# Attention scores in quarters of the array, without padded copies of q, in a fused attention and FFN kernel

## The chip, the cores and the metric

The kernel runs on one core of a Trainium2 chip. The metric is the time of one execution on the device in microseconds, as the median of several executions. A core has five engines with a queue of instructions each: TensorE (PE: matrix products and transposes, which write to PSUM), VectorE (DVE), ScalarE (ACT), GpSimd (POOL) and SyncE (SP). GpSimd and SyncE issue the DMA transfers here; GpSimd also does a few elementwise products. Engines wait for each other by semaphores.

## The reference, cut to what matters

q, k and v are 8 batches x 8 heads x 576 positions x 64 in fp32. Attention is within chunks of 64 positions; a feed-forward network (FFN) of four weight matrices follows.

```
q_c, k_c, v_c = (t.reshape(B, H, S // 64, 64, D) for t in (q, k, v))
scores = scale * np.matmul(q_c, k_c.transpose(0, 1, 2, 4, 3))
scores = scores - np.max(scores, axis=-1, keepdims=True)
attn = np.exp(scores)
attn = attn / (np.sum(attn, axis=-1, keepdims=True) + 1e-09)
out = np.matmul(attn, v_c)
x = out.transpose(0, 2, 1, 3).reshape(4608, 512)
h = (x @ w1) * (x @ w2) @ w3          # 512 -> 1024 -> 1024
return h @ w_out                      # 4608 x 512
```

## The kernel before, in words

**Groups and tiles.** The 4608 tokens are 36 groups of 128 (two chunks of 64), and the FFN works on 9 tiles of 4 groups. Matrix operands are bf16.

**One group of attention** (`add_group`). q and k of a group are loaded side by side into a tile `raw`. They must be turned, so that the head dimension lies on partitions. `TURN_QK` says how: by a DMA transpose that SyncE issues (`qk_turn`, tile `kqT`; 25 groups), or by 16 TensorE transposes into PSUM (`t_emit`, tile `p_tr`, 64 partitions per transpose; 11 groups). On the partitions of a turned tile lie two heads, 64 rows each. To get the scores of both heads from one matmul that contracts over 128 partitions, q is copied into a padded tile `qd` (three of them, zeroed at the start): the first head's q into the upper left part, the second's into the lower right (`q_copy`, two copies per group). k is used as it was turned by DMA, or copied from `p_tr` (`k_copy`). `s_emit` then does 8 matmuls of 64 columns into one PSUM bank, `p_sc`; on its partitions are the two heads, and along the row chunk, head pair and key.

VectorE takes the maximum per row (`max_emit`). Then, for most groups, VectorE subtracts it (`sub_emit`, tile `sd`) and ScalarE takes the exponential of the whole tile; for the 13 groups in `EXP_8`, ScalarE takes it straight from PSUM in 8 instructions, one per head and chunk, with the maximum as its bias (and q was scaled when it was copied). VectorE sums and inverts, and VectorE or GpSimd normalizes into `an` (five groups on GpSimd). The probabilities are turned, by DMA for 20 groups (`at_turn`) or by 4 TensorE transposes into a bank `p_at` for 16 (`at_emit`, `TURN_A`), multiplied by v (`av_emit`, 8 matmuls into `p_av`), and copied into `xt`, the input of the FFN.

**The FFN.** w3 and w_out are multiplied first (`add_w3o`: 8 transposes of a row block of w3, then 8 matmuls, for each of 8 rows), so that the FFN has two stages: `add_tile` does 64 matmuls of 512 columns with w1 and w2, ScalarE copies one product and VectorE multiplies the two (`abT`), and then 8 matmuls per group with the product of w3 and w_out give the output.

**What sets the order.** All of these are entries of a `Plan`. It walks through time with a cost for each entry, and gives each engine the ready entry with the lowest key; `SHIFT` (four numbers per group) and `ROW_KEY` move the keys. The instruction order of every engine is fixed by that. GpSimd is the exception: it takes the loads in the order of `LOADS`, in which `("an", g)` is a normalization done by GpSimd. Until 20 us of the plan, TensorE's idle time is filled with matmuls on a zero tile (`fill`). PSUM has 8 banks: 4 for `ffn`, one each for `p_sc`, `p_at`, `p_av` and `p_tr`.

Of the kernel before, what the change touches and what calls it, by code (L numbers as in the profile page):

```python
# [21 lines left out]
LOADS = [("qk", 0), ("wo", 0, 4), ("ident",), ("qk", 1), ("w3", 7, 8), ("wo", 4, 8), ("qk", 2), ("w3", 2, 3),  # L22
# [10 lines left out]
SLACK, SLACK_FROM = 1.48611, 4  # L33

TURN_QK = [g not in (0, 1, 2, 3, 4, 5, 6, 7, 8, 9, 12,) for g in range(36)]
TURN_A = [g not in (0, 1, 2, 3, 4, 5, 6, 7, 11, 13, 14, 15, 16, 21, 25, 27,) for g in range(36)]
LATE = 5
PACKED = 0.33
SHIFT = {0: (-214, -279, -160, -174), 1: (-78, -168, -88, -40), 2: (-37, -204, -55, -133), 3: (-142, -300, -25, -102),
# [10 lines left out]
ROW_KEY = [-2.1, 1.9, -1.9, 8.1, -5.5, 1, 8.1, -2.9]  # L50
EXP_8 = (2, 4, 5, 6, 7, 9, 10, 12, 13, 14, 15, 18, 19)
# [15 lines left out]
class Plan:  # L67
# [34 lines left out]
    def run(self):  # L102
        free = {e: 0.0 for e in ("PE", "ACT", "DVE", "POOL", "SP")}
        free["POOL"] = free["SP"] = 1.2
# [60 lines left out]
def kernel(  # L165
# [19 lines left out]
    nc = tc.nc  # L185
# [17 lines left out]
    BUFS = {"raw": 6, "kqT": 4, "kT": 3, "qd": 3, "vd": 3, "sd": 2, "e": 2, "an": 4, "at": 6, "w3t": 2, "abT": 2,  # L203
            "a_sb": 3, "o_sb": 4, "ffn": 4, "p_sc": 1, "p_at": 1, "p_av": 1, "p_tr": 1}
# [23 lines left out]
    qds = [wpool.tile([P, NM, 2, 2 * C], bf, tag=f"qd{i}", name=f"qd{i}") for i in range(BUFS["qd"])]  # L228
# [4 lines left out]
    plan = Plan(BUFS, ("qd", "kT", "kqT", "sd", "e", "an", "at"))  # L233

    def copy(eng, o, i, f=None):
        if f is not None:
            if eng == "ACT":
                nc.scalar.mul(o, i, f)  # L238
            else:
                nc.vector.tensor_scalar(o, i, f, None, op0=ALU.mult)  # L240
        elif eng == "ACT":
            nc.scalar.copy(o, i)  # L242
        else:
            nc.vector.tensor_copy(o, i)  # L244

    zero_q = [plan.add("DVE", 0.5, -1000 + 2 * i, lambda eng, t=t: nc.vector.memset(t[:], 0.0))  # L246
              for i, t in enumerate(qds)]
# [9 lines left out]
    eps_e = [plan.add("DVE", 0.2, -900 + i, eps_emit(t)) for i, t in enumerate(es)]  # L257
    zero_v = [plan.add("DVE", 2.0, (-999, -29, 9)[i], lambda eng, t=t: nc.vector.memset(t[:], 0.0))  # L258
# [60 lines left out]
    def load_row(r):  # L319
# [12 lines left out]
        o = plan.add("SP", 1.27, -500 + r, emit_, takes=() if r % 2 else ("abT",), lag=1.3, issue=0.3)  # L332
# [15 lines left out]
    def add_group(g, kt, ks, ka, kv):  # L348
        box = {}
        bc = chunks(g)  # L350
        qd = qds[g % len(qds)]
        e = es[g % len(es)]

        turned, by_head = TURN_QK[g], g in EXP_8

        def t_emit(eng):
            t = box["tr"] = ps("p_tr", [P, 2, 2, NM, C], bf)
            raw = raws[g]["t"].rearrange("p (s u r d) -> p s u r d", s=NM, u=2, r=2)
            for s in range(NM):
                for r in range(2):  # L360
                    for u in range(2):
                        nc.tensor.transpose(t[halves[u], r, :, s, :], raw[:, s, u, r], ident[:])  # L362

        def qk_turn(eng):
            t = sb("kqT", [P, 2 * NM, P])
            nc.sync.dma_start_transpose(t[:], raws[g]["t"][:])
            box["tr"] = t.rearrange("p (w s) t -> p w s t", w=2)
            box["kT"] = box["tr"][:, 1]
# [5 lines left out]
        def k_copy(eng):  # L374
            box["kT"] = sb("kT", [P, NM, P])
            copy(eng, box["kT"].rearrange("p s (x r) -> p (s x) r", r=2),
                 box["tr"][:, :, 1].rearrange("p r s x -> p (s x) r"))

        def q_copy(u):
            def emit(eng):  # L380
                o = qd[halves[u], :, :, u * C:(u + 1) * C]
                if turned:
                    o, i = o.rearrange("p s cc t -> p (s cc) t"), box["tr"][halves[u], 0].rearrange("p s (cc t) -> p (s cc) t", cc=2)
                else:
                    o = o.rearrange("p s cc (x r) -> p (s cc) x r", r=2)
                    i = box["tr"][halves[u], :, 0].rearrange("p r s (cc x) -> p (s cc) x r", cc=2)
                copy(eng, o, i, scale if by_head else None)
            return emit

        def s_emit(eng):  # L390
            sc = box["sc"] = ps("p_sc", [P, 2, 2, 2, C])
            for cc in range(2):
                for y in range(2):
                    for t in range(2):
                        s = y + 2 * t
                        nc.tensor.matmul(sc[:, cc, y, t, :], qd[:, s, cc, :], box["kT"][:, s, cc * C:(cc + 1) * C],  # L396
                                         start=True, stop=True)

        def flat(x):
            return x.rearrange("p cc y t k -> p (cc y t) k")  # L400

        def max_emit(eng):
            nm = box["nm"] = sb("nm", [P, 8, 1], f32, bufs=3)
            nc.vector.tensor_reduce(nm[:, :, 0], flat(box["sc"]), axis=AX.X, op=ALU.max, negate=by_head)  # L404
# [260 lines left out]
```

## Time and profile before

| what | us |
|---|---|
| median of 3 runs | 257.04 (254.79 to 258.16) |
| the profiled execution | 254.33 |
| its span, first to last instruction | 252.4 |
| TensorE busy | 239.8 (95%) |
| VectorE busy | 180.3 (71%) |
| ScalarE busy | 146.5 (58%) |
| GpSimd busy | 102.0 (40%) |

The profiled execution is one run of its own, and its time is compared with the span: 1.9 us lie around the first and the last instruction. The page gives for each engine its busy time and number of instructions (PEld are TensorE's weight loads, one per matmul), the clock granted to TensorE, and the chain of waits that ended last. Groups of instructions are listed by line, engine and operation, with what is written and read (`out<-in`), partitions x elements, the count, the busy time and the mean length of one in ns, and after the bar the idle time before them and what ended it. Matmuls overlap, so the length of one (193 ns for 64 columns) is more than the step to the next.

### The profile page before, as it was taken

Reading aid. Unit: us, or ns where it says so; the run is one execution under the profiler, and the core shown is the slowest. Engines: PE = TensorE matmul, PEld = TensorE weight load, DVE = VectorE, ACT = ScalarE, POOL = GpSimd, SP = SyncE. Lnnn points to the kernel's source line nnn. Section 1 sums busy time; section 2 is a strip of 40 time slices with the busy share of each in tenths; the row PEclk is TensorE's granted clock in tenths of the full one; section 3 lists DMA queues with packets and bytes.
Section 4 is the critical chain, followed back from the end, with each engine's and each line's share of the span. In section 5 each row is a group of like instructions: output and inputs, shape, how many; then the busy total and the mean of one; then the engine's idle time right before and its main releaser. Section 6 shows DMA issues by size and latency. Waiting matters only on the chain.

```text
span 252.4 us, 4956 instructions
## 1 busy us (share of the span) xinstructions
PE 239.8 (95%) x1836; PEld 122.4 (48%) x1836; DVE 180.3 (71%) x318; ACT 146.5 (58%) x317; POOL 102.0 (40%) x131
## 2 busy tenths in 40 slices
PE   7489997999999999999999999999999999999994
PEld 2246664554454455545554454555445545444443
DVE  7879988979999889858998586786779873222310
ACT  4448577657667776686784464575577444433232
POOL 8547797998745228600198342183000000000000
PEclk9999999999999999999999999999999999999999
DMA  8999999999999999999599999999999991121123
GB/s 205 175 202 186 167 149 176 191 165 140 156 134 156 138 155 168 134 150 146 104 86 136 149 196 158 199 181 156 179 180 228 392 258 42 42 86 42 42 83 125
DMA packets 150054, 38.85 MB, mean 154 GB/s; under 512 B 139152, under 2 KB 144528, under 8 KB 150032
## 3 DMA queue, kind: packets, MB, share of 16 engines
q0 software_dynamic: 107136, 18.88, 96.2%
q1 hardware_dynamic: 42896, 19.67, 42.6%
q8 instruction: 14, 0.23, 0.4%
q14 instruction: 8, 0.07, 0.1%
HBM read 38.80 MB, written 9.44 MB: 191 GB/s over the span
## 4 chain that ended last, share of the span: by engine, by line
PE 81%; DVE 8%; DMA 7%; ACT 2%; issue 1%; ACTq 0%; DVEq 0%
PE ffn L537 43%; PE ffn L562 22%; PE ffn L499 5%; DMA kqT<-raw 4%; PE p_sc L396 3%; PE p_av L442 3%; DMA at<-an 3%; DVE vd L258 2%; PE p_tr L362 2%; PE p_at L431 1%; DVE qd L244 1%; DVE qd L240 1%; ACT qd L238 1%; DVE qd L246 1%; PE ffn L488 1%
## 5 line engine op out<-in xcount | busy, mean ns | idle before, releaser
L537 PE MATMUL ffn<-xt,w_sb 128*128 128x512 bf16 x576 | 134.6, 379 | 0.3 <-DVE xt L244 0.3
L537 PEld LDWEIGHTS <-w_sb 128*128 128x128 bf16 x576 | 53.3, 98 | 57.5 <-issue 0.7
L546 DVE TENSOR_TENSOR abT<-a_sb,ffn 128x512 bf16<-128x512 f32 x72 | 48.9, 680 | 32.6 <-PE ffn L537 31.7
L562 PE MATMUL ffn<-w3o_sb,abT 128*128 128x512 bf16 (+1 forms) x296 | 67.6, 373 | 0.0
L242 ACT COPY a_sb<-ffn 128x512 f32<-128x512 f32 x72 | 42.4, 588 | 28.6 <-PE ffn L537 28.3
L562 PEld LDWEIGHTS <-abT 128*128 128x128 bf16 x296 | 28.4, 98 | 31.4
L283 POOL DMA_DIRECT2D raw<-in_q_dram x28 | 24.0, 860 | 21.0 <-DMA vd<-in_v_dram 8.2
L242 ACT COPY o_sb<-ffn 128x512 f32<-128x512 f32 (+1 forms) x23 | 13.1, 568 | 32.2 <-PE ffn L562 32.2
L404 DVE TENSOR_REDUCE nm<-p_sc 128x8 f32<-128x512 f32 x36 | 24.4, 678 | 7.0 <-PE p_sc L396 6.6
L420 DVE TENSOR_REDUCE ss<-e 128x8 f32<-128x528 bf16 x36 | 25.1, 698 | 5.6 <-ACT e L411 3.0
L283 POOL DMA_DIRECT2D raw<-in_k_dram x28 | 23.9, 859 | 10.9 <-DMA vd<-in_v_dram 8.8
L416 ACT ACTIVATE e<-p_sc,nm 128x64 bf16<-128x64 f32 x104 | 22.7, 332 | 1.5 <-DVE nm L404 1.4
L426 DVE TENSOR_TENSOR an<-e,rs 128x512 bf16<-128x512 bf16 x31 | 21.2, 684 | 0.2
L295 POOL DMA_DIRECT2D vd<-in_v_dram x16 | 18.7, 1192 | 5.2 <-DMA vd<-in_v_dram 2.7
L411 ACT ACTIVATE e<-sd 128x512 bf16<-128x512 f32 x23 | 14.5, 631 | 7.5 <-DVE sd L408 7.3
L396 PEld LDWEIGHTS <-qd 128*128 128x128 bf16 x288 | 12.6, 98 | 11.2 <-DVE qd L244 3.3
L242 ACT CAST xt<-p_av 128x512 bf16<-128x512 f32 x22 | 12.9, 589 | 5.9 <-PE p_av L442 5.8
L442 PEld LDWEIGHTS <-vd 128*128 128x128 bf16 x288 | 12.5, 98 | 8.1 <-DVE at L244 1.6
L442 PE MATMUL p_av<-at,vd 128*128 128x64 bf16 x288 | 14.3, 193 | 1.8 <-DVE at L244 1.4
L408 DVE TENSOR_TENSOR sd<-p_sc,nm 128x512 f32<-128x512 f32 x23 | 15.7, 684 | 0.3
L242 ACT COPY qd<-kqT 64x512 bf16<-64x512 bf16 x24 | 14.8, 617 | 2.0 <-DMA kqT<-raw 1.7
L499 PE MATMUL ffn<-wo_sb,w3t 128*128 128x512 bf16 x64 | 15.7, 380 | 0.0
(51 smaller groups left out, 186.7 us busy)
## 6 DMA issues: line engine op xcount, KB each, us to landing
out_dram<-o_sb SPq DMA_DIRECT2D x23, 256.0 KB, 3.7
vd<-in_v_dram POOLq DMA_DIRECT2D x16, 288.0 KB, 10.6
raw<-in_q_dram POOLq DMA_DIRECT2D x32, 128.0 KB, 9.8
raw<-in_k_dram POOLq DMA_DIRECT2D x32, 128.0 KB, 9.7
w_sb<-in_moe_w_dram POOLq DMA_DIRECT2D x16, 128.0 KB, 5.8
out_dram<-held_w SPq DMA_DIRECT2D x8, 256.0 KB, 4.4
w_sb<-in_moe_w_dram POOLq DMA_DIRECT2D x6, 256.0 KB, 6.8
stage<-in_moe_w_dram SPq DMA_DIRECT2D x2, 512.0 KB, 3.9
```

Of the source, the lines that this page charges most:

```text
L242: nc.scalar.copy(o, i)
L283: nc.gpsimd.dma_start(box["t"].rearrange("p (w h d) -> p w h d", w=2, h=H)[r, w], x.rearrange("h p d -> p h d"))
L396: nc.tensor.matmul(sc[:, cc, y, t, :], qd[:, s, cc, :], box["kT"][:, s, cc * C:(cc + 1) * C], start=True, stop=True)
L404: nc.vector.tensor_reduce(nm[:, :, 0], flat(box["sc"]), axis=AX.X, op=ALU.max, negate=by_head)
L416: nc.scalar.activation(e[:, i, :C], x[:, i, :], ACT.Exp, bias=box["nm"][:, i, :])
L420: nc.vector.reduce_sum(ss[:], e[:], axis=AX.X)
L426: (nc.gpsimd if eng == "POOL" else nc.vector).tensor_mul(an[:], e[:, :, :C], box["rs"].to_broadcast([P, 8, C]))
L442: nc.tensor.matmul(t[:, m, cc, :], vds[b % len(vds)][:, m, c, :], box["at"][:, 2 * cc + y, u * C:(u + 1) * C], start=True, stop=True)
L499: nc.tensor.matmul(box["wp"][:], box["t"][:, ki, :], wo_sb[:, ki, :], start=(ki == 0), stop=(ki == FO - 1))
L537: nc.tensor.matmul(t[:, :w], wt[:, ki, j * P:(j + 1) * P], x[:, ki, :], start=(ki == 0), stop=(ki == KO - 1))
L546: nc.vector.tensor_mul(box["abT"][:, j, :w], box["as", j][:, :w], box["b", j][:, :w])
L562: nc.tensor.matmul(t[:, :x1 - x0], box["abT"][:, ki, tk * P:(tk + 1) * P], w3o_sb[:, ki, x0:x1], start=(ki == 0), stop=(ki == FO - 1))
```

## The change

- `s_emit` does 16 matmuls of 64 x 64 x 64 instead of 8. Each takes 64 partitions of the turned q and k (one head of a pair, `u`) and one chunk (`cc`), and so a quarter of the array. On the partitions of the result are now the two chunks. The two heads of a pair go to two PSUM banks, and `p_sc` is two half-used banks.
- The padded tiles `qd`, their zeroing and the copies of q and k into `qd` and `kT` are gone. Groups turned by DMA need no copy at all. Groups turned by TensorE are copied from PSUM into `kqT` in two copies of 128 partitions (`kq_copy`).
- With them goes the exponential by head (`EXP_8`): all groups subtract the maximum on VectorE and take one exponential.
- `p_tr` and `p_at` become one bank, `p_t`, with one buffer for both kinds of transposes.
- `kqT` has 6 buffers instead of 4.
- A new order: another `LOADS`, `SHIFT` and `ROW_KEY`. Group 13 joins those turned by TensorE (12 groups), and 15 groups instead of 16 have their probabilities turned by TensorE. On GpSimd's queue groups 0 and 1 now stand ahead of w_out, the first piece of w1 and w2 (`("w12", 0, 2)`) comes after five groups and five rows of w3 instead of seven and six, and row 7 of w3 comes after all of w1 and w2. GpSimd normalizes six groups (2, 5, 11, 12, 15 and 21).

```diff
-LOADS = [("qk", 0), ("wo", 0, 4), ("ident",), ("qk", 1), ("w3", 7, 8), ("wo", 4, 8), ("qk", 2), ("w3", 2, 3),
-         ("w3", 4, 5), ("qk", 3), ("qk", 4), ("w3", 6, 7), ("w3", 5, 6), ("qk", 5), ("v", 0), ("an", 2), ("w3", 3, 4),
-         ("qk", 6), ("w12", 0, 2), ("v", 1), ("an", 3), ("qk", 7), ("an", 4), ("w12", 2, 4), ("w12", 4, 6),
-         ("w12", 6, 8), ("qk", 8), ("qk", 9), ("qk", 10), ("qk", 11), ("qk", 12), ("qk", 13), ("v", 2), ("qk", 14),
...
+LOADS = [("qk", 0), ("qk", 1), ("wo", 0, 4), ("ident",), ("wo", 4, 8), ("w3", 4, 5), ("w3", 2, 3), ("qk", 2),
+         ("w3", 5, 6), ("qk", 3), ("v", 0), ("w3", 3, 4), ("w3", 6, 7), ("qk", 4), ("an", 2), ("w12", 0, 2), ("qk", 5),
+         ("w12", 6, 8), ("qk", 6), ("qk", 7), ("w12", 2, 4), ("w12", 4, 6), ("qk", 8), ("w3", 7, 8), ("v", 1),
+         ("qk", 9), ("an", 5), ("qk", 10), ("qk", 11), ("v", 2), ("qk", 12), ("qk", 13), ("qk", 14), ("qk", 15),
...
-TURN_QK = [g not in (0, 1, 2, 3, 4, 5, 6, 7, 8, 9, 12,) for g in range(36)]
-TURN_A = [g not in (0, 1, 2, 3, 4, 5, 6, 7, 11, 13, 14, 15, 16, 21, 25, 27,) for g in range(36)]
+TURN_QK = [g not in (0, 1, 2, 3, 4, 5, 6, 7, 8, 9, 12, 13,) for g in range(36)]
+TURN_A = [g not in (0, 1, 2, 3, 4, 5, 6, 9, 12, 13, 15, 17, 19, 20, 24,) for g in range(36)]
...
-    BUFS = {"raw": 6, "kqT": 4, "kT": 3, "qd": 3, "vd": 3, "sd": 2, "e": 2, "an": 4, "at": 6, "w3t": 2, "abT": 2,
-            "a_sb": 3, "o_sb": 4, "ffn": 4, "p_sc": 1, "p_at": 1, "p_av": 1, "p_tr": 1}
+    BUFS = {"raw": 6, "kqT": 6, "vd": 3, "sd": 2, "e": 2, "an": 4, "at": 6, "w3t": 2, "abT": 2,
+            "a_sb": 3, "o_sb": 4, "ffn": 4, "p_sc": 1, "p_av": 1, "p_t": 1}
...
         def t_emit(eng):
-            t = box["tr"] = ps("p_tr", [P, 2, 2, NM, C], bf)
+            box["kqT"] = sb("kqT", [P, 2 * NM, P])
+            t = box["tr"] = ps("p_t", [P, 2, 4, P], bf).rearrange("p r (w s) (z x) -> p r w (s z) x", w=2, z=2)
...
-        def q_copy(u):
-            def emit(eng):
-                o = qd[halves[u], :, :, u * C:(u + 1) * C]
...
+        def kq_copy(w):
+            def emit(eng):
+                copy(eng, box["kqT"][:, w * NM:(w + 1) * NM].rearrange("p s (x r) -> p (s x) r", r=2),
+                     box["tr"][:, :, w].rearrange("p r s x -> p (s x) r"))
             return emit
 
         def s_emit(eng):
-            sc = box["sc"] = ps("p_sc", [P, 2, 2, 2, C])
-            for cc in range(2):
-                for y in range(2):
-                    for t in range(2):
-                        s = y + 2 * t
-                        nc.tensor.matmul(sc[:, cc, y, t, :], qd[:, s, cc, :], box["kT"][:, s, cc * C:(cc + 1) * C],
-                                         start=True, stop=True)
+            sc = box["sc"] = ps("p_sc", [P, 2, 2, NM, C])[:, :, 0]
+            for s in range(NM):
+                for u in range(2):
+                    for cc in range(2):
+                        c = slice(cc * C, (cc + 1) * C)
+                        nc.tensor.matmul(sc[halves[cc], u, 2 * (s % 2) + s // 2], box["kqT"][halves[u], s, c],
+                                         box["kqT"][halves[u], NM + s, c], start=True, stop=True)
...
-        def exp_by_head_emit(eng):
-            x = flat(box["sc"])
-            for i in range(8):
-                nc.scalar.activation(e[:, i, :C], x[:, i, :], ACT.Exp, bias=box["nm"][:, i, :])
...
         def at_emit(eng):
-            t = box["atp"] = ps("p_at", [P, 4, P], bf)
+            box["at"] = sb("at", [P, 4, P])
+            t = box["atp"] = ps("p_t", [P, 2, 4, P], bf)[:, 0]
...
-                                     box["at"][:, 2 * cc + y, u * C:(u + 1) * C], start=True, stop=True)
+                                     box["at"][:, 2 * u + y, cc * C:(cc + 1) * C], start=True, stop=True)
```

More of the change, by code (lines that the diff above doesn't have):

```diff
@@ L103, in run @@
         free = {e: 0.0 for e in ("PE", "ACT", "DVE", "POOL", "SP")}
-        free["POOL"] = free["SP"] = 1.2
+        free["POOL"], free["SP"] = 1.2, 0.7
         todo = {e: [o for o in self.ops if e in o.engines] for e in free}
@@ L231, with copy @@
     halves = [slice(0, C), slice(C, P)]
[L233 to L241, printed above, removed]
+    plan = Plan(BUFS, ("kqT", "p_sc", "sd", "e", "an", "at"))
+    def copy(eng, o, i):
+        if eng == "ACT":
             nc.scalar.copy(o, i)
@@ L244, in copy @@
             nc.vector.tensor_copy(o, i)
-    zero_q = [plan.add("DVE", 0.5, -1000 + 2 * i, lambda eng, t=t: nc.vector.memset(t[:], 0.0))
-              for i, t in enumerate(qds)]
     eps = 1e-9
@@ L257 @@
     eps_e = [plan.add("DVE", 0.2, -900 + i, eps_emit(t)) for i, t in enumerate(es)]
+    cold = consts.tile([P, TT], bf, name="cold")
+    plan.add("DVE", 0.1, -2000, lambda eng: nc.vector.memset(cold[:], 0.0))
     zero_v = [plan.add("DVE", 2.0, (-999, -29, 9)[i], lambda eng, t=t: nc.vector.memset(t[:], 0.0))
@@ L330, in emit_ @@
             staged[r] = stage["t"]
-        o = plan.add("SP", 1.27, -500 + r, emit_, takes=() if r % 2 else ("abT",), lag=1.3, issue=0.3)
+        o = plan.add("SP", 1.45, -500 + r, emit_, takes=() if r % 2 else ("abT",), lag=1.3, issue=0.45)
         if r % 2 == 0:
@@ L364, in qk_turn @@
         def qk_turn(eng):
-            t = sb("kqT", [P, 2 * NM, P])
+            t = box["kqT"] = sb("kqT", [P, 2 * NM, P])
             nc.sync.dma_start_transpose(t[:], raws[g]["t"][:])
-            box["tr"] = t.rearrange("p (w s) t -> p w s t", w=2)
-            box["kT"] = box["tr"][:, 1]
         def at_turn(eng):
@@ L433, in at_copy @@
         def at_copy(eng):
-            at = box["at"] = sb("at", [P, 4, P])
-            copy(eng, at[:], box["atp"][:])
+            copy(eng, box["at"][:], box["atp"])
         def av_emit(eng):
@@ L472, in add_group @@
         else:
-            at = plan.add("PE", 0.23, ka, at_emit, after=(an,), takes=("p_at",), uses=[(an, "an")], lag=0.2)
-            ac = plan.add(("DVE", "ACT"), (0.43, 0.66), ka, at_copy, after=(at,), takes=("at",), uses=[(at, "p_at")])
+            at = plan.add("PE", 0.23, ka, at_emit, after=(an,), takes=("p_t", "at"), uses=[(an, "an")], lag=0.2)
+            ac = plan.add(("DVE", "ACT"), (0.43, 0.66), ka, at_copy, after=(at,), uses=[(at, "p_t")])
         av = plan.add("PE", 0.24, kv, av_emit, after=[ac] + [o for b, _ in bc for o in v_got[b]], takes=("p_av",),
-                      uses=[(ac, "at")] + [(v_got[b][0], "vd") for b in sorted({b for b, _ in bc})], lag=0.2)
+                      uses=[(ac if TURN_A[g] else at, "at")] + [(v_got[b][0], "vd") for b in sorted({b for b, _ in bc})], lag=0.2)
         x_done[g] = plan.add(("ACT", "DVE"), (0.62, 0.68), kv, x_copy, after=(av,), uses=[(av, "p_av")])
@@ L512, in add_w3o @@
         w3o_done.append(plan.add(("ACT", "DVE"), 0.7, key, mm_copy, after=mms, uses=[(mms[0], "ffn")]))
-    cold = consts.tile([P, TT], bf, name="cold")
-    plan.add("DVE", 0.1, -2000, lambda eng: nc.vector.memset(cold[:], 0.0))
     def fill(spells):
```

55 lines of the change are left out of this document (19 added, 36 removed), and 28 rows, old and new, of tables (LOADS, SHIFT).

## The prediction

> **What bounds the kernel now.** I read first the page's busy shares, clock and chain.
>
> ```profile
> PE 239.8 (95%) x1836; PEld 122.4 (48%) x1836; DVE 180.3 (71%) x318; ACT 146.5 (58%) x317; POOL 102.0 (40%) x131
> ...
> PEclk9999999999999999999999999999999999999999
> ...
> PE 81%; DVE 8%; DMA 7%; ACT 2%; issue 1%; ACTq 0%; DVEq 0%
> ```
>
> TensorE is busy almost throughout, at full clock, and is 81% of the chain. A busy share says little where matmuls overlap, so I next take the step from one matmul's start to the next, from the TensorE rows in order of time (start, length, group):
>
> ```profile
> 20.86 0.61 PE L488 MATMUL ffn<-ident,w_sb 128*128 128x128 bf16 x8
> ```
>
> ```profile
> 43.85 1.03 PE L537 MATMUL ffn<-xt,w_sb 128*128 128x512 bf16 x4
> 44.80 0.64 PE L362 MATMUL p_tr<-ident,raw 128*64 128x128 bf16 x16
> 45.37 0.41 PE L442 MATMUL p_av<-at,vd 128*128 128x64 bf16 x8
> 45.62 1.68 PE L537 MATMUL ffn<-xt,w_sb 128*128 128x512 bf16 x7
> ```
>
> A row's length less one matmul (379, 219, 193 ns for 512, 128, 64 columns), divided by the number less one, is the step: 216 ns for 512 columns, (0.61-0.219)/7 = 56 ns for 128, 29 ns for 64. The counts come from the groups by shape:
>
> ```profile
> L537 PE MATMUL ffn<-xt,w_sb 128*128 128x512 bf16 x576 | 134.6, 379 | 0.3 <-DVE xt L244 0.3
> L562 PE MATMUL ffn<-w3o_sb,abT 128*128 128x512 bf16 x280 | 65.8, 379 | 0.0
> ...
> L442 PE MATMUL p_av<-at,vd 128*128 128x64 bf16 x288 | 14.3, 193 | 1.8 <-DVE at L244 1.4 <-DMA at<-an 0.4
> ...
> L396 PE MATMUL p_sc<-kqT,qd 128*128 128x64 bf16 x200 | 9.9, 193 | 0.6 <-ACT qd L242 0.6
> ...
> L362 PE MATMUL p_tr<-ident,raw 128*64 128x128 bf16 x176 | 7.0, 222 | 1.4 <-DMA raw<-in_k_dram 1.4
> ```
>
> Work by steps: FFN 576 x 0.216 = 124.4; output 280 x 0.216 + 16 x 0.11 = 62.2; w3 times w_out 64 x 0.216 = 13.8; transposes of w3 64 x 0.056 = 3.6; probabilities times v 288 x 0.029 = 8.4; scores (200 + 88) x 0.029 = 8.4; transposes of the probabilities 64 x 0.056 = 3.6; turning q and k on TensorE 11 x 0.67 = 7.4 (below). Sum 231.8 us. TensorE works from 1.19 to about 249.1, which is 247.9, so only **16.1 us are lost**, fillers included. Where they go, the chain in order of time shows:
>
> ```profile
> 12.00 0.41 PE p_sc L396 x8
> ...
> 40.80 2.75 PE ffn L537 x12
> ```
>
> By 40.80, the first FFN matmul, TensorE has done all of w3 (3.6 + 13.8), 7 turnings (4.7), 7 scores (1.6), 5 probability transposes (1.1) and 4 products with v (0.9): 25.7 of 39.6 us. So 13.9 us are lost before the first FFN matmul and about 2.2 in all the rest. After 41 us only fewer or cheaper TensorE instructions bring time; before it an earlier first FFN matmul does.
>
> **Scores in quarters.** Removed are 288 full-array matmuls, 36 x 8 x 0.029 = 36 x 0.232. Added are 576 of 64 columns, on a quarter of the array each, which no row of before shows. The nearest is the turning on half arrays (128*64): 16 transposes of 128 columns in 0.64 step (0.64-0.219)/15 = 28 ns, half of the 56 ns that the same columns take on the whole array, so two halves run side by side. But it pays on entering and leaving: the four FFN matmuls before it, from 43.85, would let the next start at 43.85 + 4 x 0.216 = 44.71, and the product after it starts at 45.37: 0.66 (0.67 with the slower first matmul after it) for 8 x 0.056 = 0.45 of streaming, so 0.22 for the two changes of form. The quarters come in order of s, so four different ones stand together. If four run side by side, a group costs 4 x 0.029 + 0.22 = 0.34, which is 0.11 more than now: **36 x 0.11 = +4.0 us**. Bounds: no charge for the change of form gives 0.117, -4.1 us; one quarter at a time gives 16 x 0.029 + 0.22 = 0.68, +16.3. I take 0.34, since the half-array row is the nearest and shows both effects.
>
> On this the Trainium skill, page "TensorE: Matmul & The Clock Gate", speaks with two voices. Its Part 3 says that matmuls on different tiles of the array start about 4 ns apart; its Part 1 ("Wait — 56ns, not 53.3ns?") says that starts never come closer than about 25 ns. By the first the sum stays; by the second the sixteen would take 16 x 0.025 + 0.22 = 0.62 and add 14 us. The half-array row's mean of 28 ns decides neither.
>
> **Turning.** Group 13 goes from a DMA to TensorE: +0.67. One transpose of the probabilities fewer: -0.22. Together +0.45.
>
> **VectorE and ScalarE.** Gone are the copies of q (VectorE 5.2 + 4.8 + 4.8 + 2.5 = 17.3, ScalarE 14.8 + 4.1 + 3.2 + 0.6 = 22.7), those of k (3.4; 3.5), the zeroing of the padded tiles (1.5) and the exponentials by head (104 x 0.332 = 22.7 in the listing). Added are 24 copies of 128x512 from PSUM (10 x 0.68; 14 x 0.59), 13 subtractions (13 x 0.684 = 8.9) and 13 whole exponentials (13 x 0.631 = 8.2). One normalization more (0.68) moves to GpSimd. VectorE loses 7.2 us, ScalarE 32.4. After 41 us I count that as nothing: TensorE covers it. Only the 2.2 us of late waits could go, and the shared bank makes new ones.
>
> **The start.** Here it may count, but VectorE gains least and is nearly full:
>
> ```profile
> 20.00:40.00 20.00, 18.41 (x233) 11.57 (x232) 17.90 (x33) 14.36 (x40) 17.17 (x22) 1.00 1.76 166
> ```
>
> (TensorE, weight loads, VectorE, ScalarE, GpSimd busy.) TensorE's largest wait is there too:
>
> ```profile
> PE p_sc L396 <- DVE qd L244: 2.5, 1, 2.5
> PE p_av L442 <- DVE at L244: 1.4, 1, 1.4
> ```
>
> The first was for three copies behind the zeroing, 10.1 to 12.0; now there are two, one on each engine, so group 0's scores can start near 9.5. But a filler or w_out's landing stands behind them: w_out's halves landed at 10.89 and 16.15, and with group 1 ahead of them I place them near 12 and 15. The real gain is the order of loads on GpSimd's queue. Before, seven groups, six rows of w3, w_out and a batch of v stand ahead of the first piece of w1 and w2, which landed at 37.8; now five groups, five rows, w_out and v do. Landings follow each other (1.4 us a group, 1.25 a row of w3, 0.68 a quarter of such a piece, 3.8 a batch of v), so two groups and a row fewer, 2 x 1.4 + 1.25, bring it 4 us forward, near 33.8. It still stands behind group 2's normalization on GpSimd, which in before ran at 27.07 and waited for VectorE; that keeps it from being earlier. TensorE has less to do first: 7 rows of w3 (15.2), 5 turnings (3.4), 5 scores (1.7), 4 transposes and 4 products (1.8): 22.1. With the first FFN matmul at 34.5, 33.3 - 22.1 = 11.2 are lost instead of 13.9: -2.7, of which I take **-2.5**. Bounds: -4 (at 33) and 0 (VectorE late by 2.5, so the first FFN matmul at 37).
>
> **One bank for both transposes.** A turning takes 0.66 and its copies about 1.2 with hand-over, a probability transpose 0.22 and 0.7: 2.8 us per group where a group lasts over 4. Behind a late copy stands the next transpose, and behind it in TensorE's order the FFN. Nearest rows: p_sc's waits, 0.6 and 0.4; bounds -2.2 (the late waits vanish) to +4 (one such wait for each of the first ten groups). I take 0. One row of w3 now follows all of w1 and w2 and lands near 33.8 + 4 x 1.4 + 3 x 2.7 + 1.25 = 49; TensorE reaches its transposes near 50 (34.5, then 56 FFN matmuls 12.1, 3 turnings 2.0, 3 scores 1.0, a transpose). v's second batch lands near 53, and group 4's product stands near 55. Both are just in time, and a lateness lies inside these bounds.
>
> **Sum.** 4.0 + 0.45 - 2.5 + 0 = +2.0 on the profiled execution: 254.33 to 256.3 (the span is 252.4, 1.9 lies around it). The runs' median, 257.04, is 2.7 above that execution, so I forecast 257.04 + 2.0 = **259.0**. Two per cent, 5.1 us, is about what a measurement of this kernel can tell from no change.
>
> **Rivals.**
> - Quarters are bound by their weight loads: four loads of 64 columns take a transpose's 56 ns rather than 29. A group costs 0.45, 36 x 0.11 = +4 more: 263. For it: the half-array rows never show a faster pair; against: whole-array loads keep up with 29 ns. This is the slower side; it decides from a quartet step of 50 ns (2.0 + 36 x 4 x 0.021 = 5).
> - Quarters go one after another, by the row's 28 to 29 ns: +16.3 instead of +4.0, so 271.3. For it: every whole-array row steps one matmul at a time; against: the turning's row does not. The 25 ns of the page of the Trainium skill named above would bring 259.0 + 36 x 0.28 = 269.
> - The new order waits: the shared bank at its bound of +4, 263. For it: VectorE at 17.90 of 20 us.
> - The change of form is hidden or free in quarters: 259.0 - 36 x 0.226 = 250.9, so faster. For it: a smaller tile drains less; against: every turning row in this trace pays it.
>
> **Chances.** Forecast 0.44; weight loads 0.15; one after another 0.10; order waits 0.11; free change 0.20. So faster 0.20, within 2% 0.44, slower 0.36. Range 249 to 266: it leaves out the serial case and the last part of the free one, and takes in both 263s with 3 us on them. The forecast's own range is 255 to 262.
>
> **What would show it.** Score rows of x16: from the end of the step before to the next matmul 0.34 (0.45, 0.68, 0.12 by the rivals). First FFN matmul at 34.5. TensorE's waits after it 2 us in all. ScalarE's busy time near 114, VectorE's near 173, and no effect of either on the end. The prediction is wrong if the score step is off by over 0.08 or the first FFN matmul by over 3 us.

## The result and the profile after

| | before | after |
|---|---|---|
| median of 20 runs each, us | 255.89 (254.32 to 258.16) | 257.23 (256.36 to 261.68) |
| ratio after to before | | **1.0059**, 95% interval 1.0032 to 1.0086 |
| the profiled execution / its span, us | 254.33 / 252.4 | 259.94 / 257.9 |

Medians, here and below, are of all runs, while the ratios leave out those over 1.5% above the fastest of their kernel: one of after (261.68 us), and one each of before and of the changed kernels in the experiments.

The changed kernel is 0.6% slower, some 1.5 us: more than nothing, and well within 2%. The profiled execution of after is not a typical one: 18 of the 20 runs have spans of 254.4 to 256.8 us at a granted clock of 0.997 or more, this one has 257.9 at 0.993, and where its extra time lies is shown below. That of before is not typical either: its clock was 1.000, while 38 of the 53 runs of before that were taken beside the experiments had less than 0.997. So the size of the effect is taken from the medians and ratios, and single steps from the trace.

The page of after: busy shares, clock and chain.

```profile
PE 244.6 (95%) x2105; PEld 121.2 (47%) x2142; DVE 167.6 (65%) x288; ACT 119.5 (46%) x205; POOL 102.7 (40%) x132
...
PEclk9999999979999999999999999999999999999999
...
PE 80%; DMA 8%; DVE 6%; issue 2%; ACT 2%; POOL 1%; ACTq 0%; POOLq 0%
```

TensorE bounds the kernel as before, while VectorE lost 12.7 us and ScalarE 27.0. One slice, near 55 us, has a lower clock. The score matmuls among the groups of after:

```profile
L506 PE MATMUL ffn<-xt,w_sb 128*128 128x512 bf16 x554 | 133.7, 382 | 1.5 <-issue 0.5
...
L378 PE MATMUL p_sc<-kqT 64*64 64x64 bf16 x576 | 11.5, 198 | 1.7 <-ACT kqT L236 0.7
```

The busy time of the scores, 11.5 us, is less than that of before (9.9 for 200 matmuls and 4.4 for the other 88, which read k from `kT`). But it says little, since matmuls overlap: what counts is how long TensorE is kept from the next FFN matmul. That is read from its timeline (start, length, group):

```profile
132.34 1.67 PE L531 MATMUL ffn<-w3o_sb,abT 128*128 128x512 bf16 x7
133.94 0.32 PE L378 MATMUL p_sc<-kqT 64*64 64x64 bf16 x16
134.20 3.63 PE L506 MATMUL ffn<-xt,w_sb 128*128 128x512 bf16 x16
...
46.75 4.49 PE L506 MATMUL ffn<-xt,w_sb 128*128 128x512 bf16 x20
53.55 0.62 PE L460 MATMUL ffn<-ident,w_sb 128*128 128x128 bf16 x8 [2.31 <-DMA w_sb<-in_moe_w_dram]
54.01 1.54 PE L506 MATMUL ffn<-xt,w_sb 128*128 128x512 bf16 x3
55.35 0.63 PE L409 MATMUL p_t<-ident,an 128*128 128x128 bf16 x4
55.78 1.91 PE L506 MATMUL ffn<-xt,w_sb 128*128 128x512 bf16 x4
```

**A group's scores.** Seven matmuls from 132.34 at 0.216 would let the next start at 133.85. The quarters start at 133.94, 0.09 late; the next whole matmul starts at 134.20; and that one's own step is 10 ns longer. Together 0.354 us, against 0.232 before. The records one by one show four quarters starting 3 to 4 ns apart; the second four follow 53 ns after the first, and the others at 31 ns. Of the 36 groups 33 read alike, with 0.25 us from the first quarter to the next matmul; in the other three a wait or a missing record lies between.

**The disturbed place.** TensorE stood 2.31 us for row 7 of w3 (the row that now follows w1 and w2), which landed at 53.51. Behind it four FFN matmuls took 1.91 us where they take 1.03, so they ran at half clock. The windows of after show that (a granted clock of 0.56 from 54 to 57), and the stretch in which before had VectorE at 17.90 of 20 us, where it is now busy for 14.37:

```profile
20.00:40.00 20.00, 18.22 (x247) 10.45 (x249) 14.37 (x25) 10.75 (x20) 13.63 (x22) 1.00 1.48 150
54.00:57.00 3.00, 2.90 (x14) 1.40 (x12) 1.67 (x3) 0.59 (x1) 2.50 (x3) 0.56 2.15 166
```

The remaining waits of TensorE, in its list of waits, are small. None is of a transpose for the bank that both kinds now share: the turnings (`p_t L356`) wait for their loads, and where scores wait for a copy into `kqT`, they wait for what they read:

```profile
PE ffn L460 <- DMA w_sb<-in_moe_w_dram: 2.3, 1, 2.3
PE p_t L356 <- DMA raw<-in_k_dram: 1.3, 2, 0.9
...
PE p_sc L378 <- ACT kqT L236: 0.7, 2, 0.4
```

**The sum over the profiled execution.** From the first to the last matmul TensorE took 253.5 us, 5.6 more than before (247.9). Scores 36 x 0.122 = +4.4, turning +0.45; before the first FFN matmul 12.0 us are lost instead of 13.9, so -1.9; after it 4.8 instead of 2.2, so +2.6. The last is in the main row 7 and the half clock, and by their clock most runs have no such stretch. The first FFN matmul:

```profile
35.31 1.89 PE L506 MATMUL ffn<-xt,w_sb 128*128 128x512 bf16 x8
```

### The profile page after: what moved, and what is told of

It reads as the page before. It is cut to its first block, busy times and chain, and to the rows that moved or that the text cites. A ratio compares the mean times of both kernels' runs of the same rounds, so it can differ in the third digit from the quotient of the medians.

```text
span 257.9 us, 5381 instructions
## 1 busy us (share of the span) xinstructions
PE 244.6 (95%) x2105; PEld 121.2 (47%) x2142; DVE 167.6 (65%) x288; ACT 119.5 (46%) x205; POOL 102.7 (40%) x132
## 4 chain that ended last, share of the span: by engine, by line
PE 80%; DMA 8%; DVE 6%; issue 2%; ACT 2%; POOL 1%; ACTq 0%; POOLq 0%
PE ffn L506 43%; PE ffn L531 24%; PE p_av L419 3%; PE p_sc L378 3%; PE ffn L471 3%; DMA w_sb<-in_moe_w_dram 3%; DMA raw<-in_q_dram 2%; DMA raw<-in_k_dram 2%; PE p_t L356 2%; DVE kqT L238 2%; ACT kqT L236 1%; DVE sd L390 1%; PE p_t L409 1%; POOL raw L280 1%; DVE nm L386 1%
## 5 line engine op out<-in xcount | busy, mean ns | idle before, releaser
L531 PE MATMUL ffn<-w3o_sb,abT 128*128 128x512 bf16 (+1 forms) x286 | 66.4, 373 | 0.6 <-issue 0.2
L236 ACT COPY o_sb<-ffn 128x512 f32<-128x512 f32 (+1 forms) x25 | 14.2, 569 | 40.2 <-PE ffn L531 38.2
L277 POOL DMA_DIRECT2D raw<-in_k_dram x26 | 22.6, 874 | 14.9 <-DMA vd<-in_v_dram 11.7
L277 POOL DMA_DIRECT2D raw<-in_q_dram x26 | 22.8, 878 | 12.4 <-DMA kqT<-raw 6.0
L393 ACT ACTIVATE e<-sd 128x512 bf16<-128x512 f32 x36 | 22.8, 633 | 8.7 <-DVE sd L390 7.7
L390 DVE TENSOR_TENSOR sd<-p_sc,nm 128x512 f32<-128x512 f32 x36 | 24.3, 676 | 0.3
L403 POOL TENSOR_TENSOR an<-e,rs 128x512 bf16<-128x512 bf16 x6 | 6.4, 1074 | 30.3 <-PE p_av L419 13.4
L236 ACT CAST xt<-p_av 128x512 bf16<-128x512 f32 x26 | 15.3, 588 | 6.3 <-PE p_av L419 6.3
L378 PEld LDWEIGHTS <-kqT 64*64 64x64 bf16 x576 | 7.5, 107 | 14.3 <-issue 8.5
L378 PE MATMUL p_sc<-kqT 64*64 64x64 bf16 x576 | 11.5, 198 | 1.7 <-ACT kqT L236 0.7
```

Source lines behind the costliest of these rows:

```text
L277: nc.gpsimd.dma_start(box["t"].rearrange("p (w h d) -> p w h d", w=2, h=H)[r, w], x.rearrange("h p d -> p h d"))
L378: nc.tensor.matmul(sc[halves[cc], u, 2 * (s % 2) + s // 2], box["kqT"][halves[u], s, c], box["kqT"][halves[u], NM + s, c], start=True, sto ...
L390: nc.vector.tensor_sub(heads(sd), box["sc"], heads(box["nm"]).to_broadcast([P, 2, NM, C]))
L403: (nc.gpsimd if eng == "POOL" else nc.vector).tensor_mul(an[:], e[:, :, :C], box["rs"].to_broadcast([P, 8, C]))
L531: nc.tensor.matmul(t[:, :x1 - x0], box["abT"][:, ki, tk * P:(tk + 1) * P], w3o_sb[:, ki, x0:x1], start=(ki == 0), stop=(ki == FO - 1))
```

## The experiments

All kernels are the changed kernel with one edit, the last two with two. Where the order is edited, entries are moved after the planner has fixed the rest; only for the eleven planned pairs does the planner make a new order. Each is compared with runs of the kernel before on the same chip. The last column is the difference of its ratio to 1.0059, times 255.89 us. Ratios have intervals of 0.25 to 0.6% either way, and that of the changed kernel itself is 0.27%. Both together make 1.0 to 1.6 us, the more the fewer runs a kernel had (4 to 12), and a difference under that is not established by itself.

| experiment | median us | ratio to before (95%) | against the changed kernel, us |
|---|---|---|---|
| scores twice | 261.28 | 1.0239 (1.0183 to 1.0295) | +4.6 |
| a quarter matmul ahead of each product with v | 262.65 | 1.0276 (1.0239 to 1.0313) | +5.6 |
| a whole matmul there | 258.23 | 1.0108 (1.0065 to 1.0151) | +1.3 |
| first piece of w1, w2 ahead of the normalization | 258.43 | 1.0097 (1.0063 to 1.013) | +1.0 |
| that piece later | 258.74 | 1.0103 (1.0044 to 1.0161) | +1.1 |
| exponential twice | 258.37 | 1.0123 (1.0068 to 1.0177) | +1.6 |
| row 7 of w3 earlier | 256.83 | 1.0046 (1.0018 to 1.0075) | -0.3 |
| scores on the whole array | 254.15 | 0.9941 (0.9916 to 0.9966) | -3.0 |
| row 7 earlier, five pairs of scores | 256.94 | 1.0031 (0.9992 to 1.007) | -0.7 |
| row 7 earlier, eleven planned pairs | 270.10 | 1.0561 (1.0512 to 1.061) | +12.8 |

### Do the quarters run side by side? All scores twice

```
-            for s in range(NM):
+            for s in list(range(NM)) * 2:
```

> The changed kernel with every group's 16 quarter matmuls issued twice in a row (the scores are computed twice, the second time over the first, so the output is unchanged). My theory: four quarters run side by side and step every 31 ns, and the dear part of a group's 0.35 us is the change of form, which is paid once. Then 16 more matmuls cost 4 x 0.031 = 0.125 per group, 36 x 0.125 = +4.5 us on the changed kernel: about 261.7, ratio to before near 1.023. Rival, one quarter after another: 16 x 0.029 = 0.46 per group, +16.7, ratio near 1.07. Rival, TensorE is not what sets the end: 0, ratio 1.006.

Measured +4.6 us by the ratios, +4.05 by the medians. The timeline of this kernel:

```profile
137.97 0.45 PE L378 MATMUL p_sc<-kqT 64*64 64x64 bf16 x32
138.35 1.90 PE L531 MATMUL ffn<-w3o_sb,abT 128*128 128x512 bf16 x7
```

From the first quarter to the next whole matmul 0.38 us for 32, where 16 took 0.25: sixteen more cost 0.127, and 36 x 0.127 = 4.6. So four run side by side. Of a group's 0.354 us the streaming is 0.127, and the remaining 0.227 does not grow with the number of quarters.

### Does the rest belong to the change of form? One more matmul, in quarter or in whole form

One matmul of 64 columns of zeros goes ahead of each group's product with v, into the bank that the product then overwrites: on a quarter of the array, or on all of it.

```
             t = box["av"] = ps("p_av", [P, NM, 2, C])
+            nc.tensor.matmul(t[halves[0], 0, 0, :], cold[halves[0], :C], cold[halves[0], :C], start=True, stop=True)
```
```
+            nc.tensor.matmul(t[:, 0, 0, :], cold[:, :P], cold[:, :C], start=True, stop=True)
```

> The changed kernel with one additional 64x64x64 quarter matmul of zeros ahead of every group's product with v, into a place of PSUM that this product overwrites. Nothing of the computation is changed. My theory, a change of form into the quarters and back costs about 0.22 us: 36 x (0.03 + 0.22) = +9 us on the changed kernel where the neighbours are whole-array matmuls: about 266, ratio near 1.04. Rival, the change of form is free and quarters cost their step: 36 x 0.03 = +1, ratio near 1.01.

> The same place with one additional whole-array matmul of 64 columns of zeros (128 rows, 128 columns of weights). Nothing of the computation is changed. It needs no change of form, so both theories say 36 x 0.029 = +1.0 us on the changed kernel, ratio near 1.010. The difference from the run with a quarter matmul is 36 times the price of the change of form: 8 us by my theory, 0 by the rival.

The timeline of the kernel with the extra quarter, and then that with the extra whole matmul:

```profile
100.42 1.89 PE L507 MATMUL ffn<-xt,w_sb 128*128 128x512 bf16 x8
102.24 0.21 PE L416 MATMUL p_av<-cold 64*64 64x64 bf16 x1
102.38 0.41 PE L420 MATMUL p_av<-at,vd 128*128 128x64 bf16 x8
```

```profile
102.04 1.89 PE L507 MATMUL ffn<-xt,w_sb 128*128 128x512 bf16 x8
103.77 0.19 PE L416 MATMUL p_av<-cold 128*128 128x64 bf16 x1
103.80 0.40 PE L420 MATMUL p_av<-at,vd 128*128 128x64 bf16 x8
```

Eight matmuls from 100.42 end their steps at 102.15; the quarter starts at 102.24, and the whole matmul behind it 0.14 later. In whole form nothing is late, and the next one follows after 0.03. So entering the quarter form costs 0.09 us and leaving it about 0.11 more than a whole matmul does, with 10 ns on the step after. The end of the run shows 5.6 us for the one and 1.3 for the other. The difference, 4.3 (4.4 by the medians), is less than 31 x 0.22 = 6.8 (in five places a score stood ahead, and the array was in quarter form already), and less than the 9 that was expected. A part of the steps may be swallowed by waits that shrink when TensorE comes later. In the profiled execution of the first of these two kernels the wait for row 7 is

```profile
PE ffn L461 <- DMA w_sb<-in_moe_w_dram: 0.6, 2, 0.5
```

instead of 2.3. But few runs of after have the whole of that wait, so what swallows the rest in the medians is not shown.

### What are the scores' steps worth at the end? Scores on the whole array

Eight matmuls over all 128 partitions straight from the turned tiles. This leaves out the separation of the two heads of a pair, so what it computes is another function; the number of matmuls and their form are those of before, with no copies.

```
-                for u in range(2):
-                    for cc in range(2):
-                        c = slice(cc * C, (cc + 1) * C)
-                        nc.tensor.matmul(sc[halves[cc], u, 2 * (s % 2) + s // 2], box["kqT"][halves[u], s, c],
-                                         box["kqT"][halves[u], NM + s, c], start=True, stop=True)
+                for cc in range(2):
+                    nc.tensor.matmul(sc[:, cc, 2 * (s % 2) + s // 2], box["kqT"][:, s],
+                                     box["kqT"][:, NM + s, cc * C:(cc + 1) * C], start=True, stop=True)
```

> The changed kernel with the 16 quarter matmuls of a group replaced by 8 whole-array matmuls of 64 columns straight from the turned tiles. This leaves out a part of the computation: both heads of a pair are summed in one contraction, so the scores are not those of single heads; everything else, the order, the copies, the loads, is as in the changed kernel. My theory: a group's scores fall from 0.35 to 0.23 us on TensorE, 36 x 0.12 = -4.4 us; some of it becomes waiting for loads, so -2.5 to -4.4: median 253 to 254.7, ratio 0.988 to 0.996. Rival, the quarters cost no more than the whole-array form and the loss lies in the new order: no change, ratio 1.006.

Measured -3.0 us, and 0.6% faster than the kernel before, with an interval on its own side of 1. So the form of the scores costs 3.0 us at the end, of 4.4 by steps, and all the rest of the change together gains 1.5. In this kernel's list of waits stands one that after does not have:

```profile
PE p_sc L376 <- DMA kqT<-raw: 1.5, 1, 1.5
...
PE ffn L458 <- DMA w_sb<-in_moe_w_dram: 0.9, 1, 0.9
```

TensorE comes earlier to a group whose turned tile is not there yet, and stands 1.5 us for it. That can account for the missing 1.4, but the two were not varied apart.

### Does the start count? The first piece of w1 and w2 later

The loads of groups 5 and 6 go ahead of it on GpSimd's queue. The helper moves entries of the finished order:

```
+        def ahead(ops, of):
+            for x in ops:
+                order.remove(x)
+            i = order.index(of)
+            order[i:i] = ops
+
+        ahead(raws[5]["ops"] + raws[6]["ops"], w12_ops[0][0])
```

> The changed kernel with the order of every engine kept, except that on GpSimd's queue the loads of groups 5 and 6 stand ahead of the first piece of w1 and w2, as in the kernel before. My theory: part of the change's gain is that this piece comes early. It landed at 34.9 and the first FFN matmul ran at 35.3; two groups ahead of it are 4 x 0.7 = 2.8 us, so the first FFN matmul waits until 38 or so, and the end comes 1 to 3 us later (the wait for row 7 of w3 behind it absorbs a part): ratio to before 1.008 to 1.018. Rival, the start does not count since TensorE catches up later: no change, 1.006.

Measured +1.1 us by the ratios; the medians' +1.5 holds the run of 261.46 us that the ratio leaves out. In its timeline TensorE reaches the FFN and stands for the piece, so that the first FFN matmul is at 37.2 instead of 35.3:

```profile
34.76 1.03 PE L473 MATMUL ffn<-wo_sb,w3t 128*128 128x512 bf16 x4
37.20 1.02 PE L508 MATMUL ffn<-xt,w_sb 128*128 128x512 bf16 x4 [1.41 <-DMA w_sb<-in_moe_w_dram]
38.88 1.02 PE L508 MATMUL ffn<-xt,w_sb 128*128 128x512 bf16 x4 [0.66 <-DMA w_sb<-in_moe_w_dram]
```

So 1.9 us more at the start stand beside 1.1 at the end. That points to a start that counts, if not in full, but with four runs 1.1 us is not established.

### Can the start be had earlier? The same piece ahead of the normalization

In after, GpSimd stood 4.9 us for VectorE ahead of group 2's normalization, and the piece of w1 and w2 was queued behind it:

```profile
27.64 1.04 POOL L403 TENSOR_TENSOR an<-e,rs 128x512 bf16<-128x512 bf16 x1 [4.93 <-DVE rs L399]
```

```
+        ahead(w12_ops[0], an_op[2])
```

> The changed kernel with the order of every engine kept, except that on GpSimd's queue the four loads of the first piece of w1 and w2 stand ahead of group 2's normalization instead of behind it. In the changed kernel's trace the queue waited about 5 us for VectorE there, all later loads came that much later, and TensorE waited 2.3 us for row 7 of w3 and then lost 1.7 us at half clock. My theory: the later loads come 2 to 3 us earlier, the wait for row 7 and the half clock go; the median falls by 1 to 2.5 us (to 255 to 256, ratio to before 0.995 to 1.002), and the two slow runs in ten with a lower clock go. First FFN matmul stays at 35.3, since TensorE's own work stands ahead of it. Rival, the late waits are from the shared bank or VectorE: no change, ratio 1.006.

The piece landed at 31.99 instead of 34.94, row 7 at 49.75, and TensorE no longer stood for either. It was still not faster (+1.0, not established), so the gain of 1 to 2.5 us that was expected did not come. GpSimd's timeline:

```profile
23.66 0.63 POOL L297 DMA_DIRECT2D w_sb<-in_moe_w_dram  x1 [1.30 <-DMA vd<-in_v_dram]
25.59 0.61 POOL L297 DMA_DIRECT2D w_sb<-in_moe_w_dram  x1 [1.31 <-DMA vd<-in_v_dram]
26.79 0.61 POOL L297 DMA_DIRECT2D w_sb<-in_moe_w_dram  x1 [0.59 <-DMA w_sb<-in_moe_w_dram]
28.45 0.61 POOL L297 DMA_DIRECT2D w_sb<-in_moe_w_dram  x1 [1.05 <-DMA w_sb<-in_moe_w_dram]
29.08 1.05 POOL L404 TENSOR_TENSOR an<-e,rs 128x512 bf16<-128x512 bf16 x1
```

Each of the four loads went out only when the load eight places ahead of it on this queue had landed, so the normalization ran 1.4 us later than in after. TensorE's timeline has the consequence:

```profile
30.18 0.47 PE L410 MATMUL p_t<-ident,an 128*128 128x128 bf16 x4 [1.99 <-POOL an L404]
...
31.73 1.49 PE L473 MATMUL ffn<-wo_sb,w3t 128*128 128x512 bf16 x3 [0.22 <-issue]
...
37.92 1.89 PE L508 MATMUL ffn<-xt,w_sb 128*128 128x512 bf16 x8
```

A new wait of 1.99, then a stretch at half clock (three matmuls in 1.49 instead of 0.81), and the first FFN matmul came at 37.9 instead of 35.3. A wait that was taken away at 53 us came back at 30. Six of the eight runs of this kernel had a clock of 0.993 or less, so here the profiled execution is like most.

### Is the late row 7 worth something? Row 7 ahead of group 8's loads

```
+        ahead([w3_got[7]], raws[8]["ops"][0])
```

> The changed kernel with the order of every engine kept, except that on GpSimd's queue row 7 of w3 stands ahead of group 8's loads instead of behind them. In the changed kernel's trace TensorE waited 2.3 us for this row (landed at 53.5) and then ran 3.4 us at half clock; group 8 was not used before 58. My theory: the row lands 1.4 us earlier, the wait is 1 us or less and the clock stays: in a profile without the wait 2 to 4 us less than the changed kernel's profiled 259.9, in the median 0.5 to 1.5 less (255.7 to 256.7), ratio to before 1.000 to 1.004. Rival, the wait is not typical and the median hides none of it: 1.006.

Row 7 landed at 50.16 and TensorE's wait for it fell to 0.2; no run of this kernel had a clock under 0.997. The median fell by 0.4, the ratio by 0.0013: not established, and no more than that. So the large wait of the profiled execution is not what makes the changed kernel slower: without it the ratio is still above 1 by more than its interval.

### Was ScalarE's relief worth anything? The exponential twice

```
-            nc.scalar.activation(e[:, :, :C], box["sd"][:], ACT.Exp, scale=scale)
+            for _ in range(2):
+                nc.scalar.activation(e[:, :, :C], box["sd"][:], ACT.Exp, scale=scale)
```

> The changed kernel with every group's exponential done twice (the second over the first, so the output is unchanged): 36 x 0.633 = 23 us more on ScalarE, about what the change took from it. My theory: TensorE covers ScalarE, so what the change took from ScalarE is worth next to nothing: +0 to +1 us, ratio 1.006 to 1.010. Rival, the relief of ScalarE is what paid for the dearer scores: +3 us and more, ratio above 1.017.

With ScalarE busy for 139.4 us instead of 119.5, measured +1.6 (+1.1 by the medians), between the 0 to 1 that was expected and the 3 of the rival. With an uncertainty of 1.5 either way it shuts out neither. The chain to a group's product grows by 0.63 as well, which this run does not tell from ScalarE's load. So some 20 us on ScalarE are worth little at the end, about 1 to 2 us and hardly above 3.

### Fewer changes of form? Scores of two groups in a row

The score tile has two half-used banks, so a second group's scores fit into the other halves. First, with row 7 moved as above, five groups' scores are moved straight behind those of the group before, and nothing else:

```
+    PAIRS = (14, 16, 20, 22, 24)
...
-            sc = box["sc"] = ps("p_sc", [P, 2, 2, NM, C])[:, :, 0]
+            if g - 1 not in PAIRS:
+                pair["t"] = ps("p_sc", [P, 2, 2, NM, C])
+            sc = box["sc"] = pair["t"][:, :, int(g - 1 in PAIRS)]
...
+        for g in PAIRS:
+            order.remove(s_op[g + 1])
+            order.insert(order.index(s_op[g]) + 1, s_op[g + 1])
```

> The changed kernel with row 7 of w3 ahead of group 8's loads, and with the scores of five groups (15, 17, 21, 23, 25) issued straight behind those of the group before, into the other half of the two score banks; nothing else is moved. If the charge of about 0.22 us falls on each change from whole-array to quarter matmuls and back, five changes fewer save 1.1 us of TensorE's steps beyond the version with row 7 moved alone (256.83): 255.7 (255.2 to 256.3), ratio to the kernel before 0.998 to 1.003. If the charge is part of each group's quarters themselves (a first quartet that is slow wherever it stands), nothing is saved: 256.8.

Its timeline shows the saving:

```profile
127.43 1.03 PE L513 MATMUL ffn<-xt,w_sb 128*128 128x512 bf16 x4
128.39 0.45 PE L383 MATMUL p_sc<-kqT 64*64 64x64 bf16 x32
128.77 0.41 PE L424 MATMUL p_av<-at,vd 128*128 128x64 bf16 x8
```

Entering costs 0.09 (128.39 against 127.43 + 4 x 0.216 = 128.29, and 0.093 by the records), 32 quarters 0.38, and 10 ns more: 0.48 for two groups where two single ones take 0.71. So the charge goes by changes of form, as expected. But group 21's turned tile landed late (at 120.4, 0.9 us after group 20's scores), and there TensorE stood for 0.86 amid the quarters. Four times 0.23 less 0.63 leaves 0.3; by the ratio it was 0.4 better than with row 7 alone, by the median 0.1 worse. The median lies above the 255.2 to 256.3 that were expected, and as a gain at the end this stays open.

Second, the planner was told of pairs for all groups from 14 on, one entry for the scores of both:

```
+            def both(eng):
+                t = ps("p_sc", [P, 2, 2, NM, C])
+                box0["half"], box["half"] = t[:, :, 0], t[:, :, 1]
+                emit0(eng)
+                s_emit(eng)
+
+            s = plan.add("PE", 0.35, ks0, both, after=kq0 + kq, takes=("p_sc",), uses=held0 + held_kq, lag=0.2)
```

> The same, but with all groups from 14 on in pairs (11 pairs), where the planner knows the pairs and sets a new order around them. By the charge per change of form 11 x 0.22 = 2.4 us less than 256.83: 254.4 (253.5 to 255.5), ratio 0.990 to 0.998, if the new order brings no waits of its own. Rival: the pair waits for the later of its two turned tiles and VectorE takes two groups in a burst, so that waits before the FFN tiles give the gain back: 256 to 259. If the charge does not go by changes of form: 256.8 or more.

270.10 us, far worse than even the rival's 256 to 259. The windows of this kernel (TensorE, weight loads, VectorE, ScalarE, GpSimd busy, then clock):

```profile
100.00:120.00 20.00, 19.11 (x142) 9.20 (x143) 9.85 (x17) 9.30 (x16) 6.93 (x9) 1.00 1.93 152
120.00:140.00 20.00, 13.05 (x177) 7.02 (x176) 18.58 (x36) 9.47 (x18) 11.49 (x12) 0.84 1.33 117
```

and its list of waits:

```profile
PE p_av L421 <- DMA at<-an: 5.0, 4, 2.1
...
PE p_t L411 <- DVE an L405: 2.5, 1, 2.5
PE p_sc L380 <- DVE sd L392: 2.2, 3, 1.1
```

VectorE has half its time free in one stretch and 1.4 of 20 us in the next, where three pairs' maxima, subtractions, sums and normalizations stand in bursts; TensorE is busy for 13 of 20 us there. These are waits of the kind that the rival names, but their size is not the rival's, and the largest sum is for the turned probabilities, which come by DMA. The pairs and the order that the planner made for them were not tried apart, so the cause of the loss is not shown, and the order may carry most of it.

No version with the whole computation was shown to be faster than the kernel before.

## The step of the prediction that failed, and what was right

It gave 259.0 us, and 257.23 were measured. A small loss, within 2%, was the likeliest case, and so it came out. The step that failed is the last one of the sum, from the profiled execution to the runs' median: 2.7 us were added for it, and it measured 1.6. So 259.0 lies 3.1 us above the median of before over 20 runs, twice the 1.5 that the change costs. The +2.0 of the sum itself is near that, but in part by luck: the scores cost 3.0 at the end instead of 4.0, and the rest gained 1.5 instead of 2.05, and these two errors partly cancel.

- **Scores: right by steps, too large at the end.** 0.34 us per group was forecast and 0.354 measured. The two parts of it hold one by one: streaming 0.127 (forecast 4 x 0.029 = 0.117) and the change of form 0.227 (0.22, taken from the half-array rows). The +4.0 was +4.4 by steps, and 3.0 at the end. Of the two voices of the Trainium skill, page "TensorE: Matmul & The Clock Gate", the 4 ns between different tiles in Part 3 agree with the 3.5 ns measured here; the floor of 25 ns between starts in Part 1 does not hold for matmuls on different quarters. Another of its pages, "TensorEngine Tiling (Array Packing)", section "Key Properties", says that a change of tiling mode drains TensorE; the runs fit that, and give the price, 0.22 to 0.23 us there and back.
- **Weight loads: the rival falls.** It needed 56 ns per four quarters; 31 were measured, but for 53 between the first two fours, and the 22 by which that is longer are in the 0.227. **One after another falls** with the doubled scores (4.6 us, not 16). **The free change of form falls** with the extra quarter.
- **Turning, +0.45: as forecast.** The trace has 12 turnings of 16 transposes, and in TensorE's list of waits they wait for nothing but their loads.
- **Start, -2.5: right in kind, somewhat too large.** In the profiled execution the first FFN matmul was at 35.3 instead of 34.5, and 12.0 us were lost instead of 11.2: -1.9. The piece of w1 and w2 was forecast to land at 33.8 and landed at 34.94, since GpSimd stood for VectorE until 27.6; two groups and a row fewer ahead of it gave 2.9 us of the 4 (it was at 37.8).
- **The shared bank and the late waits, 0: right for the bank, wrong for the row.** No wait on the bank shows. Row 7 was forecast at 49 and landed at 53.51: 1.1 us by the late first piece, 2.1 by the four groups and three pieces behind that (15.8 where 13.7 was added up), and 1.5 by the row itself (2.75 after the load ahead of it, for 1.25). TensorE then stood 2.31 us and ran at half clock behind it. That is +2.6 in the profiled execution, inside the bound of +4, and the largest error against that execution: it was forecast at 256.3 and took 259.94. So the rival of the waiting order came in part there, by row 7 and not by the bank. In the median it counts for little: with row 7 earlier, that moves by 0.4 only.
- **VectorE 173 and ScalarE 114: the sum right, the split wrong.** They were 167.6 and 119.5, together 287.1 against 287. The new order gave ScalarE some 5.5 us of copies that VectorE had, among them four of the 14 into `xt` and two of the four into the product of w3 and w_out. That this has no effect on the end was forecast too; the doubled exponential (+1.6, with 1.5 either way) suggests a small one.
- **From the profile to the median: the step that failed.** The sum was made against 254.33, and 2.7 was added because the median of three runs was 257.04. Over 20 runs the median of before is 255.89, 1.6 above the profiled execution. The forecast is 1.8 us too high, and 1.15 of that is this term; the rest is what +2.0 exceeds the +1.34 between the medians by. Where the 1.6 come from is open for the most part. The lower clock of most runs of before may explain some 0.6: the 38 with less than 0.997 took 256.1 us in the mean, the other 15 took 255.4. After kept its clock in 18 of 20 runs, so a part of the 1.5 that the rest of the change gains may be this; it was not tried apart.

Without the form of the scores the change gains 1.5 us (the run on the whole array); the forecast's other terms say 2.05. With it, 3.0 are lost. So where did the gain of the removed copies go? Most of them were done by engines that TensorE covered. The start gained a little under 2 us in the profiled execution, and the quarters' change of form took more than that back, 36 times. Whether the copies had a part in the gain at the start is not shown: two groups' loads put back ahead of w1 and w2 undo 1.9 us of it with all copies gone, and the kernel before with the new order of loads alone was not run.

## What to carry to other kernels

Short runs of small matmuls on parts of the array pay mostly for the change of form: here 0.227 of a group's 0.354 us. Before splitting, count how often TensorE goes there and back. Two groups in a row paid it once, though no gain at the end was shown for that; ask whether the engine that reads the results can take the burst. Copies removed from engines that the bounding engine covers bring little at the end: 39.7 us less on VectorE and ScalarE did not pay for 3.0 us on TensorE. The offset from a profiled execution to a median of three runs is itself uncertain by more than a small change; keep it out of the difference.

## What the runs showed of the hardware that was not expected

- Four quarter matmuls start 3 to 4 ns apart, and fours of them follow at 31 ns, hardly slower than one whole-array matmul of 64 columns (29 ns); the second four come 53 ns after the first.
- A change to the quarter form costs 93 ns behind a whole-array matmul, and the way back about 0.11 to 0.13 us, with the 10 ns on the step after it.
- TensorE's waits of 1.99 us (first piece moved ahead), 2.31 (after) and 2.13 (planned pairs, with another of 2.51 soon after) each came with some 3 us or more at half clock. One of 2.46 in the kernel before, at 9.5 to 12.0, did not, nor one of 2.07 in the kernel with planned pairs, at 40.3 to 42.4, nor waits of 1.4 to 1.7 in other kernels. At half clock 3 us lose about 1.5 us of work, so such a wait can cost over one and a half times its length. What decides whether the half clock comes is not shown.
- GpSimd's loads stopped at eight under way: at each of the four issues shown above, the next one was issued 0.3 us after the landing of the eighth before it. An elementwise product on that queue waits along with them. Whether the program's semaphores or the queue set the eight was not tried.
